# Block 0 of a chunked-attention and MLP kernel: turned k copied from two PSUM banks by two engines, and the first scores placed ahead of the second turn of q

## The chip, the cores and the metric

One core of a Trainium2 chip runs the whole program. The metric is the time of one execution on the device in microseconds (us). Runs of one kernel spread from about 289.5 to 292.7.

## The reference

Eight batches, eight heads, 576 tokens in chunks of 64, head size 64. Attention stays inside a chunk. Its output, 4608 rows of 512, goes through an MLP with a gate.

```python
scores = scale * np.matmul(q_c, k_c.transpose(0, 1, 2, 4, 3))
attn = np.exp(scores - max); attn = attn / sum
out = np.matmul(attn, v_c)                 # -> x [4608, 512]
h = x @ w_in                               # w_in [512, 2048]
g = h * (1.0 / (1.0 + np.exp(-beta * h)))
return g @ w_out                           # w_out [2048, 512]
```

## The kernel before

The kernel works in nine blocks of 512 rows. In each steady block TensorE alternates between the first MLP product (`mm1`), the second (`mm2`) and the attention of the next block. Block 0 is the start-up: its q and k come from memory in two halves each, are cast to bf16, turned by eight TensorE transposes into a PSUM bank, and copied to SBUF. Then follow scores, exponentials, attend, the division by the sum, a turn of x, and `mm1`. Instructions are queued in the order of a planned time:

```python
def turn_half(blk, name, half, ps, bank, eng):
    mid = ps[:, bank, :].bitcast(BF16)
    for i in range(8):
        ... e.transpose(mid[:, 128*i:128*i+128], cast[name][:, c:c+128], identity)
    copy(eng, turned[name][...], mid.rearrange("x (i p h) -> x h p i", i=8, h=4), ...)
...
for t, name, half, cast_eng, turn_t, bank, eng in (
        (4, "q", 0, "dve", 4.7, 0, "act"), (4.1, "k", 0, "dve", 6, 1, "dve"),
        (6.5, "q", 1, "pool", 7.9, 2, "act"), (6.6, "k", 1, "dve", 8.3, 3, "dve")):
    ...
for half, t, t2 in ((0, 8, 8.05), (1, 9.7, 9.75)):
    at(t - 100, scores_half, 0, half, 2 * half)      # scores at 8 and 9.7
```

The weights arrive meanwhile from one queue. GpSimd casts most of them:

```python
for e0, n in [(i, 1) for i in range(6)] + [(6, 2)]:   # w_in: 8 pieces, the last two in one DMA
    at(-97.7, load_w_in, e0, n)
for j in range(4):
    at(-97.6, load_w_out, j)
...
for e0 in range(2, 8):                                # two casts on GpSimd for each piece
    at(2 * e0 - 2.5, cast_w_in, e0, 1, ("pool", "pool"))
```

The softmax here doesn't subtract the row's maximum and nothing guards it: scores larger than these inputs give would overflow.

## Time and profile before

| | before |
|---|---|
| time, first three runs | 290.44 us median (290.42 to 291.21) |
| span of the profiled run | 288.4 us |
| TensorE busy | 278.3 us (96%) |
| first k cast to first scores | 10.39 - 7.49 = 2.90 us |
| first to second scores | 13.34 - 10.39 = 2.95 us |
| first w_out matmul | at 31.52 us |

In the profile PE is TensorE, PEld its weight loads, DVE VectorE, ACT ScalarE and POOL GpSimd. A timeline row has the start, the length, the engine, the line of the kernel, the operation, the tile written and the one read, and in brackets the idle time before and what ended it. The rows themselves stand in the prediction.

I call everything up to the first full-width `mm1` tile the front. The two marks are the tanh rows of block 0 (ScalarE, 128x512), which follow each other at 0.86 us while TensorE never waits, and the start of GpSimd's casts from the last w_in load. In this trace the last of the 14 tanh rows starts at 31.72, and the casts at 27.26: 4.46 us apart.

```profile
31.72 0.69 ACT L488 ACTIVATE tt<-F,beta_half 128x512 bf16<-128x512 f32 x1 [0.18 <-PE F L479]
```

I call these casts the gate.

### The profile page before, as it was taken

To read this page: it belongs to the slowest core of one execution; us is meant where nothing else is said; L and a number is where in the kernel's file an instruction comes from. 1 tells how busy PE (TensorE), PEld (TensorE's weight loads), DVE (VectorE), ACT (ScalarE), POOL (GpSimd) and SP (SyncE) were. 2 spreads that over 40 slices of the span, in tenths; PEclk is the share of its full clock that TensorE was granted. 3 is DMA by queue.
4 is the path that set the end of the run, shared out by engine and by line. 5 is a ranking of instruction groups with operands and counts; after the bars stand their busy time and mean duration, and the time that the engine had idled before them with its cause. 6 is when DMAs were issued, how large, how long until landed. Compare 5 with 4: busy or idle time off the path is not lost.

```text
span 288.4 us, 5455 instructions
## 1 busy us (share of the span) xinstructions
PE 278.3 (96%) x2208; PEld 140.4 (49%) x2243; DVE 148.7 (52%) x292; ACT 161.5 (56%) x233; POOL 77.4 (27%) x115
## 2 busy tenths in 40 slices
PE   5899999999999999999999999999999999999995
PEld 1654456745444544455445544554445444544444
DVE  0777436784348444844384527451856185608601
ACT  2477326877167815882588247834783387438510
POOL 1436854823230622150206020410224020000000
PEclk9799999999999999999999999999999999999999
DMA  6999999999899999895999599958989990340033
GB/s 228 262 350 395 404 332 286 248 178 246 149 273 193 275 203 236 190 232 147 239 222 195 134 237 214 222 112 206 212 165 188 208 226 2 80 135 6 0 71 74
DMA packets 134183, 57.50 MB, mean 199 GB/s; under 512 B 116624, under 2 KB 126096, under 8 KB 134160
## 3 DMA queue, kind: packets, MB, share of 16 engines
q1 hardware_dynamic: 128560, 47.33, 74.4%
q10 hardware_dynamic: 5600, 9.84, 11.2%
q8 instruction: 17, 0.28, 0.4%
q14 instruction: 6, 0.05, 0.1%
HBM read 36.71 MB, written 9.44 MB: 160 GB/s over the span
## 4 chain that ended last, share of the span: by engine, by line
PE 87%; DMA 6%; SPq 3%; issue 1%; DVE 1%; POOL 1%; POOLq 0%
PE F L523 39%; PE F L479 36%; PE A L420 2%; PE F L499 2%; DMA kstage<-in_k_dram 2%; DMA vstage<-in_v_dram 2%; DMA qstage<-in_q_dram 2%; PE A L394 2%; PE F L548 1%; SPq L306 1%; SPq L287 1%; PE F L350 1%; SPq L453 1%; PE A L350 1%; SPq L333 1%
## 5 line engine op out<-in xcount | busy, mean ns | idle before, releaser
L491 DVE SCALAR_TENSOR_TENSOR g<-tt,F 128x512 bf16<-128x512 bf16 x136 | 93.5, 687 | 71.5 <-ACT tt L488 71.3
L523 PE MATMUL F<-w_out_bf,g 128*128 128x512 bf16 x542 | 124.9, 379 | 1.7 <-issue 1.0
L479 PE MATMUL F<-xT,w_in_bf 128*128 128x512 bf16 x527 | 117.9, 379 | 0.9
L488 ACT ACTIVATE tt<-F,beta_half 128x512 bf16<-128x512 f32 x136 | 93.4, 687 | 24.5 <-PE F L479 24.3
L479 PEld LDWEIGHTS F<-xT,w_in_bf 128*128 128x128 bf16 x544 | 53.1, 98 | 64.1 <-DVE g L491 0.5
L523 PEld LDWEIGHTS F<-w_out_bf,g 128*128 128x128 bf16 x560 | 52.1, 98 | 57.3 <-POOL w_out_bf L266 0.3
L531 ACT ACTIVATE ostage<-F 128x512 f32<-128x512 f32 x33 | 19.6, 598 | 67.1 <-PE F L523 66.9
L266 POOL CAST vaug<-vstage 128x512 bf16<-128x512 f32 x35 | 21.5, 613 | 75.9 <-DMA vstage<-in_v_dram 72.1
L415 ACT ACTIVATE wstage<-A 64x1024 bf16<-64x1024 f32 x28 | 28.5, 1018 | 5.2 <-PE A L394 4.7
L266 POOL CAST qcast<-qstage 128x1024 bf16<-128x1024 f32 (+1 forms) x18 | 17.0, 945 | 44.8 <-DMA qstage<-in_q_dram 44.2
L446 DVE TENSOR_TENSOR x_sb<-A,rden 128x256 bf16<-128x256 f32 (+1 forms) x62 | 27.9, 450 | 2.1
L444 DVE RECIPROCAL rden<-A 128x4 f32<-128x4 f32 (+1 forms) x62 | 11.1, 179 | 30.6 <-PE A L420 29.4
L266 POOL CAST kcast<-kstage 128x512 bf16<-128x512 f32 (+1 forms) x29 | 18.1, 628 | 25.1 <-DMA kstage<-in_k_dram 24.8
L420 PEld LDWEIGHTS A<-vaug,wstage 128*128 128x128 bf16 x224 | 10.8, 98 | 6.6
L420 PE MATMUL A<-vaug,wstage 128*128 128x65 bf16 x224 | 11.7, 193 | 0.0
L266 POOL CAST w_in_bf<-wstage 128x512 bf16<-128x512 f32 x14 | 8.2, 613 | 7.5 <-DMA wstage<-in_moe_w_in_dram 7.5
L266 POOL CAST w_out_bf<-wstage 128x1024 bf16<-128x1024 f32 x8 | 8.1, 1040 | 1.9 <-DMA wstage<-in_moe_w_out_dram 1.9
L266 DVE CAST qcast<-qstage 128x1024 bf16<-128x1024 f32 x2 | 1.9, 934 | 12.6 <-DMA qstage<-in_q_dram 12.6
L499 PE MATMUL F<-xT,w_in_bf 128*128 128x256 bf16 x64 | 8.0, 273 | 0.2
L509 ACT ACTIVATE tt<-F,beta_half 128x256 bf16<-128x256 f32 x16 | 6.7, 470 | 2.2 <-PE F L499 2.1
L553 DVE TENSOR_SCALAR ostage<-F 128x256 f32<-128x256 f32 x2 | 0.8, 424 | 12.0 <-PE F L548 12.0
L513 DVE SCALAR_TENSOR_TENSOR g<-tt,F 128x512 bf16<-128x512 bf16 x8 | 5.5, 686 | 2.2 <-ACT tt L509 2.2
(58 smaller groups left out, 88.8 us busy)
## 6 DMA issues: line engine op xcount, KB each, us to landing
vstage<-in_v_dram SPq DMA_DIRECT2D x32, 256.0 KB, 5.2
out_dram<-ostage ACTq DMA_DIRECT2D x32, 256.0 KB, 3.4
kstage<-in_k_dram SPq DMA_DIRECT2D x30, 256.0 KB, 6.5
qstage<-in_q_dram SPq DMA_DIRECT2D x12, 512.0 KB, 5.4
wstage<-in_moe_w_out_dram SPq DMA_DIRECT2D x4, 1024.0 KB, 12.9
wstage<-in_moe_w_in_dram SPq DMA_DIRECT2D x6, 512.0 KB, 8.1
qstage<-in_q_dram SPq DMA_DIRECT2D x8, 256.0 KB, 8.6
wstage<-in_moe_w_in_dram SPq DMA_DIRECT2D x1, 1024.0 KB, 11.0
```

The lines of the kernel that those rows point to most:

```text
L266: P.op(eng, lambda e: e.tensor_copy(dst, src), reads=r, writes=wr)
L415: P.op("act", lambda e: e.activation(dst, src, AF.Exp, scale=0.125), reads=[K("A", 2 * u + i, v=("s", blk)) for i in range(2)], writes=[K( ...
L420: P.op("pe", lambda e, h=h: e.matmul(A[:, bank, 128 * (h % 4):128 * (h % 4) + 65], EB[:, 16 * u + 8 * (h % 2) + 4 * (h // 2 % 2) + m, :], ...
L444: P.op("dve", lambda e: e.reciprocal(rd, o[:, :, :, 64]), reads=r, writes=[K("rden", m, u, v=blk) for u in us])
L446: P.op("dve", lambda e: e.tensor_tensor(x_sb[:, m, 256 * us[0]:256 * (us[0] + n)].rearrange("p (b h d) -> p b h d", h=4, b=n), o[:, :, :, ...
L479: P.op("pe", lambda e, c=c: e.matmul(F[:, bank, :], w_in_bf[:, c, 256 * e0 + i:256 * e0 + 256:2], xT[:, c, :], start=(c == 0), stop=(c == ...
L488: P.op("act", lambda e: e.activation(tt[:, T % NTT, :], F[:, bank, :], AF.Tanh, scale=beta_half[:, e0, i:i + 1]), reads=[K("F", bank, v=(" ...
L491: P.op("dve", lambda e: e.scalar_tensor_tensor(g2[:, t, :], tt[:, T % NTT, :], 1.0, F[:, bank, :], ALU.add, ALU.mult), reads=[K("F", bank, ...
L499: P.op("pe", lambda e, i=i, c=c: e.matmul(F[:, bank, 256 * i:256 * i + 256], w_in_bf[:, c, 256 * pair + i:256 * pair + 256:2], xT[:, c, 25 ...
L509: P.op("act", lambda e, i=i: e.activation(tt[:, s, 256 * i:256 * i + 256], F[:, bank, 256 * i:256 * i + 256], AF.Tanh, scale=beta_half[:, ...
L523: P.op("pe", lambda e, t=t: e.matmul(F[:, s, :], g2[:, t, 128 * s:128 * s + 128], w_out_bf[:, t, :], start=(t == 0), stop=(t == NT - 1)), ...
L531: f = (lambda e: e.activation(dst, src, AF.Copy, scale=0.5)) if eng == "act" else \
```

## The change

Its intent: k of each half is ready sooner, since VectorE and ScalarE each copy half of it out of a bank of its own. The first scores no longer queue behind the second turn of q.

```diff
-        def turn_half(blk, name, half, ps, bank, eng):
+        def turn_half(blk, name, half, *parts):
+            n = 8 // len(parts)
+            for j, (ps, bank, eng) in enumerate(parts):
+                mid = ps[:, bank, 0:64 * n].bitcast(BF16)
+                for i in range(n):
+                    ... transposes n*j+i of the half into this bank
+            for j, (ps, bank, eng) in enumerate(parts):
+                copy(eng, turned[name][...][:, :, :, n * j:n * j + n], mid..., ...)
 ...
-        (4, "q", 0, "dve", 4.7, 0, "act"), (4.1, "k", 0, "dve", 6, 1, "dve"),
-        (6.5, "q", 1, "pool", 7.9, 2, "act"), (6.6, "k", 1, "dve", 8.3, 3, "dve")):
+        (4, "q", 0, "dve", 4.7, (F, 0, "act")), (4.1, "k", 0, "dve", 6, (F, 1, "dve"), (A, 2, "act")),
+        (6.5, "q", 1, "pool", 8.06, (F, 2, "act")), (6.6, "k", 1, "dve", 8.3, (F, 3, "dve"), (A, 2, "act"))):
```

The first scores have the planned time 8, so moving the second q turn from 7.9 to 8.06 puts it behind them. A further edit (not shown) makes the scores of block 0 wait for both halves of k.

More of the change, by code (lines that the diff above doesn't have):

```diff
@@ L343, in cast_half @@
                  [K(name + "cast", 2 * half + j, v=blk) for j in range(2)])
-        def turn_half(blk, name, half, ps, bank, eng):
-            key = K(*pkey(ps, bank), v=("turn", blk, name, half))
-            mid = ps[:, bank, :].bitcast(BF16)
-            for i in range(8):
-                c = 1024 * half + 128 * i
-                P.op("pe", lambda e, i=i, c=c: e.transpose(
-                    mid[:, 128 * i:128 * i + 128], cast[name][:, c:c + 128], identity[:, :]),
-                    reads=[K("identity")] + [K(name + "cast", 2 * half + x, v=blk) for x in range(2)],
-                    writes=[key])
-            copy(eng, turned[name][:, :, 256 * half:256 * half + 256].rearrange("x h (p i) -> x h p i", i=8),
-                 mid.rearrange("x (i p h) -> x h p i", i=8, h=4),
-                 [key], [K(name + "T", hp, half, v=blk) for hp in range(4)])
+        def turn_half(blk, name, half, *parts):
+            n = 8 // len(parts)
+            for j, (ps, bank, eng) in enumerate(parts):
+                key = K(*pkey(ps, bank), v=("turn", blk, name, half))
+                mid = ps[:, bank, 0:64 * n].bitcast(BF16)
+                for i in range(n):
+                    c = 1024 * half + 128 * (n * j + i)
+                    P.op("pe", lambda e, i=i, c=c, mid=mid: e.transpose(
+                        mid[:, 128 * i:128 * i + 128], cast[name][:, c:c + 128], identity[:, :]),
+                        reads=[K("identity")] + [K(name + "cast", 2 * half + x, v=blk) for x in range(2)],
+                        writes=[key])
+            for j, (ps, bank, eng) in enumerate(parts):
+                key = K(*pkey(ps, bank), v=("turn", blk, name, half))
+                mid = ps[:, bank, 0:64 * n].bitcast(BF16)
+                copy(eng, turned[name][:, :, 256 * half:256 * half + 256].rearrange(
+                    "x h (p i) -> x h p i", i=8)[:, :, :, n * j:n * j + n],
+                    mid.rearrange("x (i p h) -> x h p i", i=n, h=4),
+                    [key], [K(name + "T", hp, half, *((j,) if j else ()), v=blk) for hp in range(4)])
         def scores_half(blk, half, bank0):
@@ L368, in f @@
                                             turned["k"][r, hp, t], turned["q"][r, hp, t])
-                        P.op("pe", f, reads=[K("qT", hp, half, v=blk), K("kT", hp, half, v=blk)],
+                        P.op("pe", f, reads=[K("qT", hp, half, v=blk), K("kT", hp, half, v=blk)] +
+                             ([K("kT", hp, half, 1, v=0)] if blk == 0 else []),
                              writes=[K("A", bank0 + h2, v=("s", blk))])
@@ L627, in bass_chunk_attention__then__act_swish_beta_kernel @@
             at(-97.4, load, 1, "v", m)
-        for t, name, half, cast_eng, turn_t, bank, eng in (
-                (4, "q", 0, "dve", 4.7, 0, "act"), (4.1, "k", 0, "dve", 6, 1, "dve"),
-                (6.5, "q", 1, "pool", 7.9, 2, "act"), (6.6, "k", 1, "dve", 8.3, 3, "dve")):
+        for t, name, half, cast_eng, turn_t, *parts in (
+                (4, "q", 0, "dve", 4.7, (F, 0, "act")), (4.1, "k", 0, "dve", 6, (F, 1, "dve"), (A, 2, "act")),
+                (6.5, "q", 1, "pool", 8.06, (F, 2, "act")), (6.6, "k", 1, "dve", 8.3, (F, 3, "dve"), (A, 2, "act"))):
             at(t - 100, cast_half, 0, name, half, cast_eng)
-            at(turn_t - 100, turn_half, 0, name, half, F, bank, eng)
+            at(turn_t - 100, turn_half, 0, name, half, *parts)
         for half, t, t2 in ((0, 8, 8.05), (1, 9.7, 9.75)):
@@ L658, in bass_chunk_attention__then__act_swish_beta_kernel @@
             at(tc, cast_half, 1, name, half, ceng)
-            at(tt_, turn_half, 1, name, half, A, bank, eng)
+            at(tt_, turn_half, 1, name, half, (A, bank, eng))
         for half, ts in ((0, 28.95), (1, 30.93)):
```

## The prediction

> **What bounds the kernel now.** I began with the page's totals and slices, to see how much of the span the changed stage can own at all.
>
> ```profile
> span 288.4 us, 5455 instructions
> PE 278.3 (96%) x2208; PEld 140.4 (49%) x2243; DVE 148.7 (52%) x292; ACT 161.5 (56%) x233; POOL 77.4 (27%) x115
> PE   5899999999999999999999999999999999999995
> PEclk9799999999999999999999999999999999999999
> PE 87%; DMA 6%; SPq 3%; issue 1%; DVE 1%; POOL 1%; POOLq 0%
> ```
>
> TensorE is busy for 96% of the span, and only the first two slices (7.2 us each) show it neither full nor at full clock. The change touches instructions between about 8 and 14 us only. A 2% change is 5.8 us, so no outcome of this edit should reach it; the question is a few tenths of a microsecond.
>
> Second, the chain that ended last, in order of time, for that stage (start, length, what):
>
> ```profile
> 8.29 1.05 POOL qcast L266
> 9.38 1.03 PE F L350 x8
> 10.41 0.62 PE A L367 x19
> 11.03 1.01 PE F L350 x8
> 12.06 1.23 DVE kT L266
> 13.34 0.45 PE A L367 x32
> 19.44 10.95 PE F L479 x49
> ```
>
> The eight transposes (L350) of the second half of q stand in front of the first scores (L367). The second scores wait for VectorE's 1.23 us copy of k.
>
> Third, the timeline, for the durations (start, length, engine, line, operation):
>
> ```profile
> 8.28 1.02 ACT L264 ACTIVATE qT<-F 128x1024 bf16<-128x1024 bf16 x1 [4.36 <-PE F L350]
> 9.11 1.23 DVE L266 COPY kT<-F 128x1024 bf16<-128x1024 bf16 x1 [0.94 <-PE F L350]
> 11.37 1.08 ACT L373 ACTIVATE E<-A 128x512 bf16<-128x512 f32 x2
> 14.89 0.60 ACT L264 ACTIVATE xT<-F 128x512 bf16<-128x512 bf16 x1
> 15.75 0.69 DVE L446 TENSOR_TENSOR x_sb<-A,rden 128x512 bf16<-128x512 f32 x1
> ```
>
> The first k copy ends at 9.11 + 1.23 = 10.34; the q transposes ahead of the scores end at 10.41. So the two gates of the first scores end within 0.07 us of each other, and neither half of the change would help the first scores alone.
>
> Fourth, and decisive, I followed the stage forward to the point where something independent of it ends last:
>
> ```profile
> 27.26 2.29 POOL L266 CAST w_in_bf<-wstage 128x512 bf16<-128x512 f32 x4 [1.53 <-DMA wstage<-in_moe_w_in_dram]
> 28.48 2.71 PEld L479 LDWEIGHTS F<-xT,w_in_bf 128*128 128x128 bf16 x14 [0.37 <-POOL w_in_bf L266]
> 28.06 0.69 ACT L488 ACTIVATE tt<-F,beta_half 128x512 bf16<-128x512 f32 x1 [0.18 <-PE F L479]
> 29.13 0.69 ACT L488 ACTIVATE tt<-F,beta_half 128x512 bf16<-128x512 f32 x1 [0.38 <-PE F L479]
> 31.90 8.79 PEld L523 LDWEIGHTS F<-w_out_bf,g 128*128 128x128 bf16 x42 [0.28 <-POOL w_out_bf L266]
> ```
>
> GpSimd idles 1.53 us until the last w_in load lands at about 27.24, then casts it in four pieces. The second piece ends at 27.26 + 2 x 0.57 = about 28.43, and TensorE loads the weights it makes at 28.48. The tanh rows show that this costs time already: they follow each other at 0.86 us (27.20 to 28.06), but here at 29.13 - 28.06 = 1.07. TensorE stalls here for 0.21 us, which the chain of waits hides inside its row "19.44 10.95 PE F L479". At 31.90 the same happens with w_out: the weights are ready only just in time (the matmul starts at 31.95). Those loads stand in one queue from 10.5 us on and wait for nothing that the change touches.
>
> **What the Trainium skill says.** Page "ScalarE: Activation LUTs", section "What ACT_TABLE_LOAD costs": an ACTIVATE with immediate scale takes 186 ns + 0.833 ns per element, and neighbours overlap by about 93 ns. The trace agrees: 1.02 us for 1024 elements, 0.60 for 512 (the formula: 1.04 and 0.61), and two exponentials in 1.08 instead of 1.20. Page "PSUM — Partial Sum Buffer", "Specifications (TRN2)": ScalarE and VectorE read PSUM side by side at full rate if their banks differ. The change uses different banks; the trace of before has no such pair of copies to test it with. Page "TensorE: Matmul & The Clock Gate", Part 1, "What's actually happening": the array runs at half clock after an idle window of some 3.4 us and returns to full after a busy one; the windows run freely. The trace agrees in kind: granted clock 0.98 in 8.0 to 8.5 us, 0.50 until 11.5, 0.61 in the next half and 1.00 from 12.0, so low for about 3.4 us. What share of idle time in a window keeps the clock low is not shown.
>
> **The change part by part.** Times are us from the span's start, by the durations above.
>
> Split of the first k copy. Removed: one VectorE copy of 1.23. Added: a VectorE copy of 512 columns, an estimate of 0.70 (half the 1024-column part, as the 512-column operation of 0.69 confirms), and a ScalarE copy of 512, 0.60. VectorE's half starts after four transposes, about 8.65, and ends near 9.35. ScalarE's half queues behind the q copy (8.28 to 9.30), starts with the usual overlap at about 9.18 and ends at 9.78. That is the later one: k is ready at 9.78 instead of 10.34, 0.56 earlier.
>
> Scores ahead of the second q turn. The scores start at 9.83 instead of 10.39, take 0.64 at the low clock and end at 10.47. The exponentials, before at 11.37 because the second q copy held ScalarE until 11.47, now start at about 10.58 and end at 11.66. The second q turn moves from 9.38 to 10.47, and TensorE now idles from 9.07 to 9.83, 0.76 instead of 0.31.
>
> What is given back. The 16 transposes of both second turns, at about 0.107 each until 11.9 and 0.056 after, end near 12.1, against 12.02 before: TensorE has lost its early start on q. ScalarE must then do in order: exponentials to 11.66, second q copy to 12.56, second half of k to 13.04. So the second scores start at 13.09 instead of 13.34: **0.25 earlier**. VectorE's part, 11.8 to 12.5, is beside this, and VectorE is free at 12.5 instead of 13.28, so the first reciprocal can run as soon as the attend ends at about 13.0 (before 13.20). From there the chain (exponentials, attend, reciprocal, multiply, turn of x, first MLP matmuls) has the same pieces; I carry **-0.20** through, since fillers on TensorE and the w_in cast on ScalarE (16.33, its data landed near 16.05) each cap it near there. L479 starts at 19.24 instead of 19.44.
>
> What that is worth. From 19.24 TensorE runs 0.86 per tile: by 28.1 it would need the second cast piece 0.20 earlier, but it is still made at 28.43. The stall becomes 0.21 + 0.20 = 0.41, and the matmul starts at 28.49 as before. The gain on the path that sets the end: 0.20 - 0.20 = **0.00**. The same gate absorbs a delay of up to 0.21.
>
> **Rivals.**
> A. The early gain survives, -0.20 to -0.25: 290.2. For it: the page's chain follows TensorE unbroken from 19.44. Against: the widened tanh spacing of 1.07 and the cast behind a DMA. It would need the last w_in load to land sooner.
> B. The low clock stays longer, because TensorE idles 0.45 us more in the window of about 8.5 to 11.9. Then everything from 11.9 to about 15.3 runs slow: an estimate of twice the 0.64 to 0.43 difference of the filler pairs, plus some 0.2 each on scores, attends and turns, near 1.0 in all; less 0.20 won and 0.21 of slack, +0.6: 291.0. For it: the clock did fall after 1.86 us of idling. Against: the window would still be over three quarters busy (3.41 - 0.76 = 2.65 of 3.41).
> C. ScalarE becomes the bound of the stage: it gains two copies of 0.60. If they run slower than 0.60 with their scattered columns, or the exponentials queue behind them, the second scores come at 13.3 to 13.5. Slack of 0.21 absorbs it: 290.4 to 290.5.
>
> **Range and chances.** My centre is the time before, 290.4: gain 0.0. The three runs of before spread from 290.42 to 291.21, so a median may move by a tenth or two without cause. A, at some 15%, gives 290.2; C, with the main line, 290.4 to 290.5; B, at some 12%, reaches 291.0. The range that should hold it 8 times in 10 is 290.0 to 290.9. Faster by over 2%: 0.003. Slower by over 2%: 0.007. Within 2%: 0.99.
>
> **What would show the steps right or wrong.** Right: in the timeline, two k copies of about 0.70 (VectorE) and 0.60 (ScalarE) side by side, the first scores near 9.8, exponentials near 10.6, second scores near 13.1, L479 near 19.2; then a wider gap between the tanh rows around 28 us (about 1.27 in place of 1.07) and the w_in weights loaded at 28.48 again. Wrong: the w_in cast of the last load starting earlier than 27.2, or TensorE reaching it with no stall; a granted clock of 0.50 after 12 us (rival B); a ScalarE half copy well over 0.60 (rival C). The total is wrong if the time leaves 290.0 to 290.9, above all if L523 starts before 31.5 us.

## The result and the profile after

After: 290.56 us median of six runs (289.96 to 291.30); before, six runs: 290.50 (289.90 to 291.21). The ratio is 1.000 with a 95% interval of 0.9977 to 1.0022. Ratios here are the mean time of one kernel's fast runs over that of the other's in the same rounds, so not quite the ratio of the medians quoted.

The page of after, the same parts as those shown of before:

```profile
span 288.3 us, 5493 instructions
PE 279.5 (97%) x2243; PEld 139.2 (48%) x2243; DVE 148.0 (51%) x292; ACT 162.6 (56%) x235; POOL 77.7 (27%) x115
PE   5799999999999999999999999999999999999995
PEclk9999999999999999999999999999999999999999
PE 94%; DMA 2%; ACT 1%; DVE 1%; issue 0%; SPq 0%; DVEq 0%
```

ScalarE has two more instructions, the k copies. TensorE's count rises only because the trace of before lacks some matmul records. One accidental difference matters later: the clock was full here in the second slice, where before showed 7.

The chain of after in order of time, in the changed stage (start, length, what):

```profile
9.51 0.58 PE A L373 x32
10.09 1.07 ACT E L380 x2
11.16 0.92 ACT qT L264
12.08 0.50 ACT kT L264
12.58 0.14 issue
12.71 0.45 PE A L373 x32
```

Between the first and the second scores the chain now lies wholly on ScalarE: exponentials, second q copy, its half of the second k. In before, TensorE's transposes and VectorE's k copy stood in these places. The two first copies of k in the timeline:

```profile
8.23 0.69 DVE L266 COPY kT<-F 128x512 bf16<-128x512 bf16 x1 [0.49 <-PE F L352]
8.77 0.59 ACT L264 ACTIVATE kT<-A 128x512 bf16<-128x512 bf16 x1
```

They last what was estimated, and ScalarE's ends last. Then the weights and the tanh rows of after, from its timeline:

```profile
19.71 1.18 POOL L266 CAST w_in_bf<-wstage 128x512 bf16<-128x512 f32 x2 [2.12 <-DMA wstage<-in_moe_w_in_dram]
20.53 0.69 ACT L495 ACTIVATE tt<-F,beta_half 128x512 bf16<-128x512 f32 x1 [0.17 <-PE F L486]
21.82 0.69 ACT L495 ACTIVATE tt<-F,beta_half 128x512 bf16<-128x512 f32 x1 [0.60 <-PE F L486]
...
26.92 2.30 POOL L266 CAST w_in_bf<-wstage 128x512 bf16<-128x512 f32 x4 [1.52 <-DMA wstage<-in_moe_w_in_dram]
28.14 2.71 PEld L486 LDWEIGHTS F<-xT,w_in_bf 128*128 128x128 bf16 x14 [0.37 <-POOL w_in_bf L266]
28.79 0.69 ACT L495 ACTIVATE tt<-F,beta_half 128x512 bf16<-128x512 f32 x1 [0.25 <-PE F L486]
31.38 0.69 ACT L495 ACTIVATE tt<-F,beta_half 128x512 bf16<-128x512 f32 x1 [0.18 <-PE F L486]
```

TensorE reached the third w_in piece before its cast was done and stalled for 21.82 - 20.53 - 0.86 = 0.43 us, then for 0.07 at the last load. Its last tanh row starts at 31.38, and 31.38 - 26.92 = 4.46 us after the casts from the last load, as before. The first w_out matmul came at 31.18 instead of 31.52, which is the 0.34 us by which that load landed earlier in this run. That lead was lost again later: between 184 and 213.7 us this trace took 29.72 us for a block instead of 29.49. So 0.1 us remains of 0.34 in the span.

### The profile page after: what moved, and what is told of

Read it like the earlier page. It is cut to its first block, busy times and chain, and to the rows that moved or that the text cites. A ratio compares the mean times of both kernels' runs of the same rounds, so it can differ in the third digit from the quotient of the medians.

```text
span 288.3 us, 5493 instructions
## 1 busy us (share of the span) xinstructions
PE 279.5 (97%) x2243; PEld 139.2 (48%) x2243; DVE 148.0 (51%) x292; ACT 162.6 (56%) x235; POOL 77.7 (27%) x115
## 4 chain that ended last, share of the span: by engine, by line
PE 94%; DMA 2%; ACT 1%; DVE 1%; issue 0%; SPq 0%; DVEq 0%
PE F L530 42%; PE F L486 41%; PE A L427 2%; PE F L506 2%; PE A L401 2%; DMA qstage<-in_q_dram 2%; PE F L555 1%; ACT qT L264 1%; PE A L352 1%; PE A L441 1%; PE A L373 1%; PE F L469 1%; PE F L478 1%; ACT E L380 0%; ACT kT L264 0%
## 5 line engine op out<-in xcount | busy, mean ns | idle before, releaser
L530 PE MATMUL F<-w_out_bf,g 128*128 128x512 bf16 x560 | 128.5, 379 | 0.0
L486 PE MATMUL F<-xT,w_in_bf 128*128 128x512 bf16 x544 | 119.1, 379 | 0.3 <-issue 0.3
L266 POOL CAST kcast<-kstage 128x512 bf16<-128x512 f32 (+1 forms) x29 | 18.2, 631 | 24.2 <-DMA kstage<-in_k_dram 23.3
```

The source lines that it names most:

```text
L266: P.op(eng, lambda e: e.tensor_copy(dst, src), reads=r, writes=wr)
L486: P.op("pe", lambda e, c=c: e.matmul(F[:, bank, :], w_in_bf[:, c, 256 * e0 + i:256 * e0 + 256:2], xT[:, c, :], start=(c == 0), stop=(c == ...
L530: P.op("pe", lambda e, t=t: e.matmul(F[:, s, :], g2[:, t, 128 * s:128 * s + 128], w_out_bf[:, t, :], start=(t == 0), stop=(t == NT - 1)), ...
```

## The experiments

Theory: the casts behind the w_in loads set when block 0's `mm1` ends, whatever the front does within a few tenths. Rivals: the gain of the front is an accident of clock or loads; only one half of the change works; something else than the casts sets the end.

Marks of all traces, in us. Low windows are stretches of 3.4 us with a granted clock of 0.50 between 8 and 16 us. "Stalls" is the excess of the 13 tanh intervals over 0.8625 each. "Gate" is the last tanh row's start less the start of the casts from the last w_in load; more than 4.47 without stalls means that the front came later than the gate. "Open" means casts that no longer wait for their loads, "other loads" that the last load is another one. "q ahead" is the start of the first k cast less that of the first q cast: at about 0.6 the copy of q still holds ScalarE when its half of k is turned.

| trace | low windows | q ahead | first k cast to first scores | first to second scores | both | stalls | gate |
|---|---|---|---|---|---|---|---|
| before | 1 | 0.61 | 2.90 | 2.95 | 5.85 | 0.22 | 4.46 |
| before_again | 1 | 2.28 | 2.70 | 2.95 | 5.65 | 0.40 | 4.46 |
| before_nogate | 1 | 2.45 | 2.85 | 2.93 | 5.78 | 0.01 | open |
| before_finer | 0 | 0.62 | 2.68 | 2.54 | 5.22 | 0.09 | other loads |
| before_warm | 0 | 0.61 | 2.69 | 2.54 | 5.23 | 0.40 | 4.46 |
| after | 0 | 0.61 | 2.46 | 3.20 | 5.66 | 0.51 | 4.46 |
| after_again | 2 | 2.16 | 2.57 | 3.55 | 6.12 | 0.04 | 4.47 |
| after_nogate | 1 | 1.87 | 2.15 | 3.21 | 5.36 | 0.01 | open |
| after_finer | 0 | 0.65 | 2.52 | 3.22 | 5.74 | 0.47 | other loads |
| after_warm | 0 | 2.37 | 2.15 | 3.21 | 5.36 | 0.02 | 4.67 |
| after_gate_late | 1 | 2.04 | 2.15 | 3.21 | 5.36 | 1.71 | 5.59 |
| after_delay_big | 2 | 0.61 | 2.56 | 3.55 | 6.11 | 0.02 | 8.10 |
| split_only | 2 | 2.36 | 3.05 | 2.75 | 5.80 | 0.02 | 4.69 |
| order_only | 1 | 1.72 | 2.69 | 3.79 | 6.48 | 0.02 | 4.95 |

### Both kernels again

No edit. One execution each, with a trace.

> The kernel before, unchanged, for a second trace, since TensorE ran at half clock for 3.4 us (8.5 to 11.9 us) in the first trace of before and at full clock throughout in that of after. Measure: from the start of VectorE's first q cast to the start of VectorE's last xT copy (the front). In the first traces it was 17.86 - 6.88 = 10.98 us before and 17.23 - 6.44 = 10.79 after. Theory (the change shortens the front by about 0.2, whatever the clock): 10.9 to 11.0 again. Rival (the 0.19 was the clock's, not the change's): with a full clock in this stretch the front of before is 10.5 to 10.8. Stall before the w_in cast of the last load: tanh rows near 28 us 1.0 to 1.3 apart in place of 0.86, by the theory of the gate.

> The kernel after, unchanged, for a second trace. Theory: the front is 10.8 us at either clock, because ScalarE's chain (q copy, half of k, exponentials, q copy, half of k) sets it and not TensorE; the sum of the stalls in the tanh rows between 19 and 31 us is larger than in before by what the front gained. Rival (clock): with a half clock in the stretch from 8 to 12 us the front is 11.0 or more.

Measured: 291.05 and 291.12 us, one run each. The measure I had chosen, from the first q cast, failed: q's first half landed 1.5 us earlier relative to the other loads in before_again than in the first trace (first q cast at 5.35 instead of 6.88, second q cast at 8.43 instead of 8.29), so the front by that measure is 12.68 us and says nothing. I therefore count from the first k cast. The gate held in both: 4.46 and 4.47, with stalls of 0.40 and 0.04. The stalls did not grow by what the front gained, as the second text expected. The clock rival turned out real: in after_again the clock stayed at half for two windows. This is the busy time per stretch of after_again (start and end, length, then busy time of TensorE, its weight loads, VectorE, ScalarE and GpSimd with counts, then the granted clock, the DMA share and GB/s):

```profile
8.50:9.00 0.50, 0.47 (x5) 0.48 (x6) 0.00 (x0) 0.00 (x0) 0.50 (x1) 0.50 1.24 298
9.50:10.00 0.50, 0.06 (x1) 0.00 (x0) 0.46 (x2) 0.40 (x1) 0.01 (x1) 0.50 1.35 228
14.50:15.00 0.50, 0.50 (x26) 0.47 (x18) 0.48 (x1) 0.28 (x1) 0.00 (x0) 0.50 1.06 313
```

TensorE idled from 9.5 to past 10.3 us, waiting for k, and the clock was still at 0.50 at 15 us. The front was then so late that the stall shrank to 0.04, and the end of the stage, counted from the casts, still did not move.

### Each half of the change alone

split_only, against after:

```diff
-                (6.5, "q", 1, "pool", 8.06, (F, 2, "act")),
+                (6.5, "q", 1, "pool", 7.9, (F, 2, "act")),
```

> The split copies of k without the new order: the second turn of q stands before the first scores again. Worked out from the durations of before: first scores at about 10.4 us on the clock of the trace of before, since the q turn ends there, exponentials 11.4 to 12.4 as before, ScalarE's half of the second k 12.4 to 13.0, second scores at about 13.0 instead of 13.34: the front 10.6 to 10.7 us. If so the split carries the whole gain of the front. Rival (both parts needed): front 10.9 to 11.0. Time by the theory of the gate: 290.2 to 290.8, ratio 0.999 to 1.001 either way.

order_only, against before:

```diff
-                (6.5, "q", 1, "pool", 7.9, 2, "act"),
+                (6.5, "q", 1, "pool", 8.06, 2, "act"),
```

> The new order without the split: the scores still wait for the whole 1.23 us copy of k, and the second q turn now waits behind them. Worked out: second q copy on ScalarE ends near 13.1, second turn of k near 12.5, its copy near 13.7, second scores near 13.8 instead of 13.34: the front 11.3 to 11.5 us, longer than before by 0.3 to 0.5. Theory of the gate: TensorE had stalled 0.21 anyway, so the time grows by 0.1 to 0.3 at most, 290.5 to 290.8. Rival (no gate, the front goes to the end in full): 290.8 to 291.0.

Measured: split_only 290.33 us (ratio 0.9985, 0.9939 to 1.0031), order_only 290.77 (1.0014, 0.9967 to 1.006). Both times are inconclusive. In the traces, the order alone lengthens the way from the first k cast to the second scores to 6.48 us against 5.65 to 5.85 of before at the same number of low windows: its first to second scores take 3.79, and its front passes the gate late (4.95 without a stall). That is a loss, as expected, but of 0.6 to 0.8 where 0.3 to 0.5 was expected. The split alone has two low windows in its trace and cannot be held against before. It can be held against after with two (after_again, after_delay_big): its first scores come 0.5 later (3.05), but the second follow after 2.75 instead of 3.55, so the way to the second scores is 0.3 shorter (5.80 against 6.12 and 6.11). By these traces, one of split_only, the new order loses time at the second scores both with the split and without it.

### The gate taken away

In both kernels, with a wrong result:

```diff
+                if e0 > 1:
+                    st, at, s = wstage[:, 0, :].rearrange("p (c f) -> p c f", c=4), 0, 0
                 dst, src = w_in_bf[:, c, 256 * e0:256 * e0 + w], st[:, c, at:at + w]
...
-                     wstage[:, 4 + j, 512 * n * i:512 * n * (i + 1)],
+                     wstage[:, 0, 512 * n * i:512 * n * (i + 1)],
```

The keys (the names by which an instruction waits for another) are changed along with them.

> The kernel before with the gate taken away and a wrong result on purpose: the casts of w_in from the third piece on, and all casts of w_out, read the weights that were loaded first (landed by 17.5 us) instead of their own loads; the loads still run. GpSimd then makes the weights long before TensorE needs them. Theory of the gate: the stall of 0.21 us at 28.3 us goes, all tanh rows from 21 to 31 us are 0.86 apart, and the first w_out matmul comes 0.2 earlier relative to the first q cast (31.52 - 6.88 = 24.64 becomes 24.4). Rival (the stall had another cause): 24.6 as before. Time: 290.2 to 290.4.

> The same with the kernel after. Theory: with the gate gone the gain of the front, about 0.2 us, goes through to the first w_out matmul: from the first q cast 24.2 us, 0.2 less than with before_nogate, and it stands there in place of the stalls of 0.43 and 0.07 us that the tanh rows of after show. Rival (the front's gain was the clock's alone): the same 24.4 as before_nogate at equal clock. Time against before_nogate: 0.0 to 0.3 less; the spread of runs (290 to 291.3) may hide it.

Measured: before_nogate 290.44 us (ratio to before 0.9994, 0.9961 to 1.0027), after_nogate 289.95 (0.9984, 0.9949 to 1.0019). The stalls vanished from both traces (0.01), but that shows little. The last w_in load still ran, and landed at 27.16 and 26.59 us. In before it landed at 27.21, 4.51 us ahead of the last tanh row; with the gate in place that row could thus have started at 31.67 and 31.10 here, and it started at 31.82 and 31.19. Both fronts were later than the gate would have been, so these traces would have had no stall at the last load either way. The first w_out matmul came 26.22 and 25.50 us after the first q cast, where 24.4 and 24.2 were expected; that mark had failed already (above). Whether the front's gain then reaches the end is not settled: the means of the six runs, 290.13 against 290.45, lean that way, but single runs spread over 2 us. From the first k cast to the first w_out matmul the traces give 30.99 - 7.36 = 23.63 after and 31.62 - 7.85 = 23.77 before, a difference smaller than the scatter of the loads.

### Finer loads

In both kernels, with a right result:

```diff
-        for e0, n in [(i, 1) for i in range(6)] + [(6, 2)]:
+        for e0, n in [(i, 1) for i in range(8)]:
...
+            if j == 0:                     # first w_out load as two DMAs of 512 KB
+                for x in range(2):
+                    P.dma("sp", lambda e, x=x: part(e, x), writes=[K("ws", 4 + j, x)])
```

> The kernel before with the gate opened in a right way: the last w_in load (two pieces in one DMA) is issued as two, and the first w_out load as two halves with the cast of each waiting for its own half. Result right. Theory: the last-but-one piece of w_in lands near 25.7 instead of 27.2 and the first half of w_out near 28.5 instead of 29.8; no stall at 28.3; the first w_out matmul 0.2 earlier: 24.4 us after the first q cast. Rival (smaller loads make the queue slower): pieces land no earlier, 24.6. Time 290.2 to 290.4.

> The kernel after with the same finer loads. Theory: the stall near 28 us goes, but the earlier gate at the third piece of w_in (near 20 us, the 0.43 us stall of the trace of after) stays, so the first w_out matmul is 24.3 to 24.4 us after the first q cast, about as with before_finer, and the time 290.1 to 290.4. If the front's gain passes the third piece too: 24.2 us and 290.0 to 290.2.

Measured: before_finer 290.13 us (0.9984, 0.9953 to 1.0015), after_finer 290.30 (0.999, 0.9957 to 1.0023). The last-but-one piece was cast from 25.68 and the first half of w_out from 28.45 in before_finer, as expected, and no stall near 28 us was left in either trace. In after_finer the earlier gate at the third piece remained: 0.46 us there. The last tanh row came 3.85 and 3.87 us after the first cast from the last w_in load (31.03 - 27.18, 31.53 - 27.66), less than 4.46: this gate no longer held the stage. The absolute numbers counted from the first q cast (24.71 and 25.81) miss for the reason given above. Neither time beats before clear of noise.

### The full clock in both

In both kernels, more filler matmuls before the first turn:

```diff
-        at(-99.2, spin, 11, A, 3)
+        at(-99.2, spin, 17, A, 3)
```

> The kernel before with 17 instead of 11 filler matmuls at its start, so that TensorE hardly idles before the first q turn and the clock stays full. The traces so far: from the first k cast to the second scores before took 5.65 to 5.85 us where one low-clock window of 3.4 us fell into the stretch, 5.22 with the full clock (before_finer). Theory (at full clock before needs no help: VectorE and ScalarE share the copies evenly): 5.2 us again. Rival (5.22 was the arrival of the loads): 5.6 to 5.8. The time stays within noise, 289.9 to 290.9, since the cast of the last w_in load sets the end of the stage either way: the last tanh row of block 0 starts 4.46 us after that cast starts, or later if the front is late.

> The kernel after with the same 17 fillers. Theory: ScalarE's chain (exponentials, second q copy, second half of k: 1.08 + 1.02 + 0.60 less two overlaps, and two hand-overs) takes 3.2 us between the first and the second scores at any clock, so from the first k cast to the second scores 5.7 us as in after and after_finer, 0.4 to 0.5 longer than before_warm: at full clock the change makes the front longer, and only with one low-clock window shorter. Rival (the gain of 0.25 that was predicted holds at any clock): 4.9 to 5.1. Time 289.9 to 290.9 and the 4.46 us as in before_warm.

First k cast and scores in the timeline of before_warm, and then of after_warm, here with a later row of TensorE:

```profile
7.56 0.69 DVE L266 CAST kcast<-kstage 128x1024 bf16<-128x1024 f32 x1
10.25 0.45 PE L367 MATMUL A<-qT,kT 64*64 64x64 bf16 x32 [0.18 <-DVE kT L266]
12.79 0.45 PE L367 MATMUL A<-qT,kT 64*64 64x64 bf16 x32 [0.21 <-DVE kT L266]
```

```profile
7.67 0.69 DVE L266 CAST kcast<-kstage 128x1024 bf16<-128x1024 f32 x1 [1.68 <-DMA kstage<-in_k_dram]
9.82 0.44 PE L373 MATMUL A<-qT,kT 64*64 64x64 bf16 x32 [0.78 <-ACT kT L264]
13.03 0.45 PE L373 MATMUL A<-qT,kT 64*64 64x64 bf16 x32 [0.60 <-ACT kT L264]
17.70 0.61 PE L506 MATMUL F<-xT,w_in_bf 128*128 128x256 bf16 x4 [0.87 <-POOL w_in_bf L266]
```

The first k casts start at 7.56 and 7.67, and the clock was 1.00 in every stretch. So at full clock the change brings the first scores 0.54 us forward (2.15 against 2.69) and gives 0.67 back before the second (3.21 against 2.54). The sum is 0.13 longer, not 0.4 to 0.5: I had taken 5.7 from traces in which the first q copy still occupied ScalarE when k arrived (2.46 to 2.52 in after and after_finer). The two warm traces differ in this (q ahead by 0.61 and 2.37 us). With q ahead by about 0.6 in both, the full-clock traces are after and after_finer (5.66, 5.74) against before_finer and before_warm (5.22, 5.23): there the change is longer by 0.43 to 0.52. With one low window the traces of after have 5.36 (q early) against 5.65 to 5.85 of before, so there the change is shorter by 0.3 to 0.5; those windows do not begin at the same point, and the nearest pair (before_again and after_nogate, 2.8 and 2.9 us after the first k cast) gives 0.3.

The gate of 4.67 in after_warm is not the doing of the scores. Its first w_in load landed late (GpSimd cast it at 17.03, in before_warm at 15.87), and TensorE waited 0.87 us for that cast in front of the first MLP product. So an early w_in load can be a gate too; the prediction named it only as a cap on the gain, at 16.33 us.

The times were 290.84 us (1.0016, 0.9992 to 1.004) and 291.59 (1.0028, 1.0004 to 1.0053); the second lies above the expected 289.9 to 290.9, and its interval above 1. Both traces lost time later. The first tanh rows of successive blocks are 30.62 and then 29.49 us apart in an undisturbed trace; in before_warm they took 0.94 us more from 51 to 142 us, in after_warm 1.07 more from 82 to 142. TensorE waited there for DMA transposes (0.46 at 66.5 and 0.26 at 111.1; 0.80 at 111.5). Why those were late with more fillers, or whether by chance, stays open.

### The gate moved, and the front moved

after_gate_late, against after, makes GpSimd cast one piece twice:

```diff
+        at(9.4, cast_w_in, 6, 1, ("pool", "pool"))
         for e0 in range(2, 8):
```

> The kernel after with GpSimd casting the last-but-one piece of w_in twice, so that the gate opens two casts (about 1.15 us) later; the front is untouched, the result right. Theory of the gate: the last tanh row of block 0 starts 5.6 instead of 4.46 us after GpSimd's first cast from that load, the stall near 28 us grows by the same, and the time by about 1.1 us: 291.3 to 291.8. Rival (the gate doesn't set the end of the stage): 4.46 to 4.6 and 290.3.

The timeline of after_gate_late:

```profile
27.35 3.42 POOL L266 CAST w_in_bf<-wstage 128x512 bf16<-128x512 f32 x6 [1.52 <-DMA wstage<-in_moe_w_in_dram]
30.35 0.69 ACT L495 ACTIVATE tt<-F,beta_half 128x512 bf16<-128x512 f32 x1 [1.51 <-PE F L486]
32.94 0.69 ACT L495 ACTIVATE tt<-F,beta_half 128x512 bf16<-128x512 f32 x1 [0.18 <-PE F L486]
```

Six casts in place of four, a wait of 1.51 us in front of one tanh, and the last row at 32.94 - 27.35 = 5.59 us. In the trace the two casts go through in full (5.59 - 4.46 = 1.13). The time is 291.61; its ratio is to before in the same rounds, 1.0036 (1.0008 to 1.0065), which is 1.05 us with an interval of 0.2 to 1.9. The casts set the end of this stage.

after_delay_big, against after, puts ten fillers on TensorE:

```diff
+        at(0, spin, 10, A, 3)
```

> The kernel after with ten more filler matmuls (10 x 0.216 = 2.16 us) on TensorE between the first two MLP tiles and the third: the front is 2.16 us longer, the loads and casts are untouched. Theory: of these the stalls that the gates made (0.04 to 0.5 us in the traces) are absorbed first, the rest goes through: last tanh row 6.1 to 6.6 us after the first cast from the last w_in load, no stalls in the tanh rows, time longer by 1.6 to 2.1 us: 291.9 to 292.4. Rival (the gate absorbs any front delay of this size, or work downstream catches up): 4.46 and under 291.

```profile
26.71 2.29 POOL L266 CAST w_in_bf<-wstage 128x512 bf16<-128x512 f32 x4 [1.52 <-DMA wstage<-in_moe_w_in_dram]
34.81 0.69 ACT L495 ACTIVATE tt<-F,beta_half 128x512 bf16<-128x512 f32 x1 [0.18 <-PE F L486]
```

Measured: 293.36 us (1.0097, 1.0066 to 1.0128) where 291.9 to 292.4 was expected, and 8.10 us in the trace where 6.1 to 6.6 was expected. The miss has its parts. The trace is almost that of after_again up to the fillers (first k cast at 7.78 and 7.77, last copy of turned x at 18.99 and 18.98, both with two low windows), but its last w_in load landed 28.19 - 26.71 = 1.48 us earlier. So 4.47 + 1.48 + 2.16 = 8.11. Here the front was behind the gate, and the fillers came through in full. Its two runs with a mean clock of 1.000 and 0.994 took 292.62 and 292.78, the two with 0.987 and 0.988 took 294.15 and 293.94. One low window costs 0.5 x 3.41 / 288 = 0.006 of the mean clock, so by this measure the latter had two, and were some 1.3 us slower. Not all of this is the clock's: the traced one of them lost 0.44 us between 85 and 144 us, where TensorE waited for a DMA transpose (0.26 us at 113.4). How much the low windows cost once the gate no longer hides them is not shown.

## Why the prediction was right

The total was right: 290.4 predicted, 290.56 measured, and no difference to before clear of noise. Alone it says little, since noise would hide a gain of 0.2 too, and at the full clock there was no gain at the second scores for the gate to absorb. By its steps:

- **The gate.** Right, and the most firmly shown. The last tanh row stood 4.46 or 4.47 us after the casts from the last w_in load in all four traces of the two kernels as given and in before_warm, with fronts of quite different length. In the first pair the front of after was 0.29 us earlier against these casts (first full-width tanh row at 26.92 - 19.66 = 7.26 ahead of them, before 27.26 - 20.29 = 6.97), and the stalls were larger by the same 0.29 (0.51 and 0.22). Moving the casts moved the last row (5.59). The stall to come was put at 0.41; the trace of after has 0.51, but before itself has 0.40 in two other traces. The place was wrong: the gap near 28 us was 0.93 instead of 1.27, and 0.43 of the stall fell at the third w_in piece, a gate that the prediction did not name.
- **First scores 0.56 earlier.** The half copies took 0.69 and 0.59 us, as estimated. The gain agrees only by luck: 0.54 in the warm pair, whose q came early in after_warm, so that ScalarE's half did not queue behind the q copy. With q ahead by 0.6 us, the case that was worked out, it is 0.16 to 0.23 at full clock (2.46 and 2.52 against 2.68 and 2.69); at the low clock no such pair of traces exists. The hand-over was too small in my sum: 0.05 us was assumed from ScalarE to TensorE, and 9.36 to 9.51 in after is 0.15.
- **What is given back.** The chain was right, ScalarE's. The size, a net gain of 0.25 at the second scores, holds only in part: it is 0.3 to 0.5 with one low window, and at full clock a loss of 0.13 (q early) to 0.52 (q ahead by 0.6). The failing step is that before was taken from a single trace with a low window. There the first to second scores took 2.95 us, but 2.54 at full clock, while after takes 3.21 in both cases. The marks of after came out near those predicted: from the first k cast to the second scores 5.66 us against 13.09 - 7.49 = 5.60, and to the first full-width `mm1` tile 18.60 - 7.05 = 11.55 against 19.24 - 7.49 = 11.75. The first pair of traces gave -0.19 for the front, which looked like a confirmation of -0.20, but that pair compares a low clock before with a full clock after, and other arrivals of loads.
- **Signs and small slips.** Two of the prediction's own signs of being wrong appeared: the casts from the last load began before 27.2 us (26.92), and L523 before 31.5 (31.18). Both were set from the start of the span, and that load landed 0.34 us earlier in this run; counted from it nothing moved. 27.26 + 2 x 0.57 is 28.40, not 28.43; the second cast ran from 27.82 for 0.61 us. The last of the 40 slices is not full either (5). The wait for w_out at 31.90 cost nothing: its matmuls follow each other without a break (31.52, 31.74, 31.95).
- **Rival A**, the gain going to the end, is not what happened. That it would with the gate gone is not shown; the means of the nogate pair only lean that way.
- **Rival B**, a longer low clock. I gave it 12% because a window three quarters busy would do. That argument was wrong: windows in which TensorE was busy for 2.28 to 2.86 of 3.41 us kept the low clock. It did occur, and cost nothing visible at the end of the stage in after_again (4.47). Among the runs of before in the last group, mean clocks of 0.987 and 0.988 occur as well, so it is not peculiar to the change; whether the change makes it more frequent stays open.
- **Rival C**, ScalarE as the bound of the stage, is what the traces show between the two scores (3.20 to 3.22 us in five traces, without slower copies). The second scores were not as late as it said (13.3 to 13.5): 12.71, or 13.15 if counted from the first k cast of before.

## What to carry to other kernels

Before shortening a start-up chain, follow it forward to the first thing that does not depend on it, and look for a widened interval in a regular row of instructions: a stall of 0.2 us there said that a gain in front would be worth nothing in this kernel until that gate moved. Splitting a copy over two engines helped the first user here and could hurt the second, because the helper already had a chain of its own. Anchor a comparison of traces at a gate that is the same in both, not at the first instruction, and compare only at equal clock and equal arrival of the loads. A stall that vanishes when a gate is removed is evidence only if the front would have reached that gate early.

## What the Trainium skill lacked or had wrong

- "TensorE: Matmul & The Clock Gate", Part 1, "What's actually happening", says that a busy window of about 3.4 us releases the clock, not how busy it must be. Here nine low windows with TensorE busy for 3.08 us or more of 3.41 (90%) were followed by the full clock, and three with 2.28, 2.63 and 2.86 us (67 to 84%) by a second low one. Nor need the window that lowers the clock be idle: in the nine stretches of 3.41 us just before a first low window TensorE was busy for 1.17 to 1.78 us (34 to 52%). The windows' length, 3.41 us, agrees with the page.
- "ScalarE: Activation LUTs", "What ACT_TABLE_LOAD costs": the durations agree (0.59 to 0.62 us for 512 elements), but the section gives no hand-over to TensorE. The first scores followed the end of ScalarE's k copy by 0.13 to 0.15 us (9.36 to 9.51, 12.58 to 12.71), and in before_warm that of VectorE's by 0.05 (10.20 to 10.25, 12.74 to 12.79).
- "PSUM — Partial Sum Buffer", "Specifications (TRN2)": nothing wrong. In after_nogate VectorE's copy (8.54 to 9.23) and ScalarE's (8.77 to 9.37) read two banks side by side for 0.46 us and took 0.69 and 0.60; a later one of ScalarE with VectorE idle took 0.62 (11.96 to 12.58). No trace has VectorE's half alone.
